# A transformer block on one core: how the MLP's normalised rows of token blocks 1 to 3 are transposed

## The chip, the cores and the metric

The kernel runs on one core of one Trainium2 chip. A core has five engines, each with an instruction queue of its own that is worked off in order: TensorE (PE in the profile; its weight loads are listed as PEld), VectorE (DVE), ScalarE (ACT), GpSimd (POOL) and SyncE (SP), which here issues nearly all DMAs. Engines wait for one another by semaphores. TensorE reads SBUF and writes PSUM; DRAM is reached by DMA only.

The metric is the device time of one execution in microseconds (us), as the median of several executions. Before the change it is 1103.45 us (three executions, 1102.35 to 1103.99).

## The reference

All tensors are float32; there are 2048 tokens of width 448.

```python
x = A_x
mod = (_silu(c) @ w_mod).reshape(c.shape[0], 6, 1, -1)
sa, ca, ga, sb, cb, gb = (mod[:, 0], mod[:, 1], mod[:, 2], mod[:, 3], mod[:, 4], mod[:, 5])
h = _layernorm(x, axis=-1) * (1 + ca) + sa
x = x + ga * _A_ref(h, A_wqkv, A_wo)          # softmax attention, 16 heads of 28
h = _layernorm(x, axis=-1) * (1 + cb) + sb
x = x + gb * _B_ref(h, B_w1, B_b1, B_w2, B_b2)
# _B_ref: y = layernorm(h); gelu(y @ w1 + b1) @ w2 + b2, with 1792 hidden units
```

The change lies in the MLP `_B_ref` at the end, between its layernorm and its first matmul. That matmul contracts over the 448 features, and TensorE contracts over partitions, so the normalised rows, which lie with one token per partition, have to be transposed to one feature per partition.

## The kernel before, in words

The kernel works in token blocks of 512 (`NB` = 4 of them, b = 0 to 3), each held as four tiles of 128 tokens, t = 0 to 3. The layernorms, projections and attention fill the first 790 us; the MLP of the four blocks follows. Each float32 operand is split into two float32r parts, a rounded `hi` and the remainder `lo`, and each product is made as three matmuls.

**The MLP loop.** The order of every engine's instructions is that in which the program is written out; there is no scheduler. The loop runs over `seq`, 56 pairs (b, i) with i = 0 to 13, one per 128 hidden units, one number n after another. A step of it emits:

- `mlp1(b, i)`: 11 matmuls of 512 columns (line 396) over the block's transposed rows `yT[b]`, in the order hi of chunks 0 to 2 twice each, lo of chunks 0 to 2, then chunk 3 twice; a GELU on ScalarE (L1394); the split into `hi` (L1397) and `lo` (L1398). The `hi` is made by ScalarE in block 0 and by VectorE in blocks 1 to 3.
- in block 0 also the rest of the attention's output projection (`tail`, with L1032) and one or two `w_prep.step()`, which load and split weight pieces (L1175 to L1209).
- one stage of the layernorm of the next block, `lnst[b + 1][0](i)`.
- `mlp2` of the step before the last (`LAG` = 2): 12 matmuls of 448 columns (L1438 to L1440) that add into four PSUM tiles. Its last step of a block, emitted at step 1 of the next block, adds the residual (L1444) into `xn` tiles and stores them (L1445).

**The layernorm of the next block** (`ln2_stages(b)`). Its `stage(i)` takes these parts at these steps: `stat(0, t)` (statistics of the block's rows) at i = t; `mid(t)` at 4 + t, which normalises into a tile of the four-buffer ring `xn` and has GpSimd multiply and add two modulation rows; `stat(1, t)` at 6 + t; `fin(t)` at 10 + t // 2, which normalises again in place (`normalise`, L217) and copies the last 64 columns a second time behind the 448 (L1129), so that the row has four full chunks of 128; `addb(t)` at 10 + t, a GpSimd addition that prepares the residual.

**The transposes** (`chunk(k)`, k = 0 to 3). At the last step of a block (i = 13, `ahead`) chunks 0 and 1 of the next block are emitted ahead of `mlp2`, chunks 2 and 3 behind it; the next instruction on TensorE is then `mlp1(b + 1, 0)`. A chunk is four TensorE transposes of 128x128 (`transposes`, L277) into a PSUM tile, a ScalarE copy that rounds to `hi` (L1155), and a VectorE subtraction that leaves `lo` (L1157, or L1159 for chunk 3, where the 64 doubled features hold `lo` in the other half of the partitions). Since TensorE's queue is in order, `mlp2` of the last two steps of block b stands behind `mlp1(b + 1, 0)` and `mlp1(b + 1, 1)`.

`slot("e1", ...)` names an SBUF buffer that holds weights of the output projection until that is done, at step 8 of block 0 at the latest.

Of the kernel before, what the change touches and what calls it, by code (L numbers as in the profile page):

```python
# [13 lines left out]
F32 = mybir.dt.float32  # L14
F32R = mybir.dt.float32r
AF = mybir.ActivationFunctionType
ALU = mybir.AluOpType
# [5 lines left out]
D = 448  # L23
# [3 lines left out]
NC = 4  # L27
# [17 lines left out]
def tile_adaln_block(ctx: ExitStack, tc: tile.TileContext, x, wqkv, wo, w1, b1, w2, b2, c, w_mod, out):  # L45
    nc = tc.nc
    pe, act, dve, pool, sp = nc.tensor, nc.scalar, nc.vector, nc.gpsimd, nc.sync
# [13 lines left out]
    def ps_tile(key, n=1):  # L61
        return ps_pools[key][1].tile([128, 512], F32, tag=key, name=nm(key), bufs=n)
# [7 lines left out]
    dr = ctx.enter_context(tc.tile_pool(name="dr", bufs=1, space=DRAM))  # L70
# [4 lines left out]
    def nm(t):  # L75
        uid[0] += 1
        return f"{t}_{uid[0]}"

    def sbt(tag, shape, dt=F32, bufs=1):
        return sb.tile(shape, dt, tag=tag, name=nm(tag), bufs=bufs)  # L80

    def slot(tag, shape, dt=F32R):
        return sb.tile(shape, dt, tag="slot_" + tag, name=nm("slot_" + tag), bufs=1)
# [24 lines left out]
    def ps_mx():  # L108
        mx_ring.append(mx_ring.pop(0))
        return ps_tile(mx_ring[-1], 1 if mx_ring[-1] == "m1" else 2)  # L110

    def ps_o():
        return ps_tile("o")
# [4 lines left out]
    def f(t):  # L118
        return t.bitcast(F32)
# [48 lines left out]
    def mod_part(k, j, n):  # L168
        if k < 3:
            return slice(0, 128), slice(j * D, (j + 1) * D)  # L170
        h, j = divmod(j, n // 2)
        return slice(64 * h, 64 * h + 64), slice(j * D, (j + 1) * D)
# [25 lines left out]
    def ln_stat(mv, t, src):  # L198
        st = sbt("st", [128, 6], bufs=2)
        dve.bn_stats(out=st, in_=src)  # L200
        dve.bn_aggr(out=mv[:, t, :], in_=st)

    def ln_rstd(mv, n):
        ve = sbt("ve", [128, 4], bufs=2)
        dve.tensor_scalar(out=ve[:, :n], in0=mv[:, :n, 1], scalar1=EPS, scalar2=None, op0=ALU.add)
        rs = sbt("rs", [128, 4], bufs=2)
        pool.tensor_tensor(out=rs[:, :n], in0=ve[:, :n], in1=neg_half[:, :n], op=ALU.pow)
        return [(mv[:, t, 0:1], rs[:, t : t + 1], rs) for t in range(n)]
# [7 lines left out]
    def normalise(dst, src, mr):  # L216
        dve.tensor_scalar(out=dst[:, :D], in0=src, scalar1=mr[0], scalar2=mr[1], op0=ALU.subtract, op1=ALU.mult)  # L217

    def xn_t():
        return sbt("xn", [128, 512], bufs=4)  # L220
# [54 lines left out]
    def transposes(p, xs, k):  # L275
        for t in range(4):
            pe.transpose(p[:, t * 128 : (t + 1) * 128], xs[t][:, k * 128 : (k + 1) * 128], ident)  # L277
# [40 lines left out]
    for k in range(NC):  # L318
        for j in range(2):
            rs_, cs = mod_part(k, j, 2)  # L320
# [94 lines left out]
    def qk_task(b, kind, g, begun=None):  # L415
        p, ts = begun or qk_terms(b, kind, g)
        if begun is None:
            mm_acc(p, ts, p1_n[3])
        emit_task(*p1_n[:3])
        if g == 0:  # L420
            tg = ("kh" if kind else "qh") + str(b)
            hi = sb.tile([128, 512], F32R, tag=tg, name=nm(tg), bufs=1)
            (kh_sb if kind else qh_sb)[(g, b)] = hi
        elif g == 1 and b < 2:

            hi = sbt("raw" if kind else "osb", [128, 512], F32R, bufs=3 if kind else 2)
            (kh_sb if kind else qh_sb)[(g, b)] = hi
        else:
            hi = sbt("hi", [128, 512], F32R, bufs=3)
        full = sbt("full", [128, 512], bufs=3)  # L430
        lo = sbt("lo", [128, 512], F32R, bufs=3)
        act.copy(full, p)

        def split():
            (act.copy if b else dve.tensor_copy)(hi, full)
            if kind == 1 and (g, b) == (0, 1):
                k_diff.append(sbt("raw", [128, 512], F32R, bufs=3))
                pool.tensor_tensor(out=k_diff[0], in0=f(hi), in1=f(kh_sb[(0, 0)]), op=ALU.subtract)
            pool.tensor_tensor(out=lo, in0=full, in1=f(hi), op=ALU.subtract)
            sl = slice(b * 512, (b + 1) * 512)  # L440
            for part, t in enumerate((hi, lo)):
                sp.dma_start(f(dscr[kind][part][g])[:, sl], f(t))

            if b < 3 or g == 0 or (kind, g) == (0, 1):
                put_spare()
            spare.append((kind, g, sl))

        return split
# [285 lines left out]


    rows = {}
    drow = dr.tile([4, D], F32, tag="drow", name="drow", bufs=1)

    mod = {}
# [65 lines left out]
    for n, i in (  # L805
# [7 lines left out]
        p, ts = firsts[n]  # L813
# [3 lines left out]
    for b in range(NB):  # L817
# [12 lines left out]
        for n, (tb, kind, g) in enumerate(tasks):  # L830
# [9 lines left out]
            k = n - (6, 4, 4, 4)[b]  # L840
# [5 lines left out]
            if kind < 2:  # L846
                fn = qk_task(tb, kind, g, firsts[n] if b == 0 and n < 3 else None)
# [12 lines left out]
            if more:  # L860
                k = n - (6, 4, 4, 4)[b]

                if b == 0 and n in (0, 1, 3, 4):
                    x = 2 * n if n < 2 else 2 * n - 2
# [237 lines left out]
    yT = {}  # L1102

    def ln2_stages(b):
        h2 = []
        ys = []

        mv = {}
        mr = {}

        def stat(which, t):
            if t == 0:
                mv[which] = sbt("mv", [128, 4, 2], bufs=2)
            ln_stat(mv[which], t, acc[b][:, t, :] if which == 0 else h2[t])
            if t == 3:
                mr[which] = ln_rstd(mv[which], 4)

        def mid(t):
            yt = xn_t()
            ys.append(yt)  # L1120
            y = yt[:, :D]
            normalise(y, acc[b][:, t, :], mr[0][t])
            pool.tensor_tensor(out=y, in0=y, in1=rows["cb"], op=ALU.mult)
            pool.tensor_tensor(out=y, in0=y, in1=rows["sb"], op=ALU.add)
            h2.append(y)

        def fin(t):
            normalise(ys[t], h2[t], mr[1][t])
            dve.tensor_copy(ys[t][:, D:512], ys[t][:, 384:D])  # L1129

        def addb(t):
            pool.tensor_tensor(out=acc[b][:, t, :], in0=acc[b][:, t, :], in1=rows["b2g"], op=ALU.add)

        plan = {}
        for t in range(4):
            plan.setdefault(t, []).append(lambda t=t: stat(0, t))
            plan.setdefault(4 + t, []).append(lambda t=t: mid(t))
            plan.setdefault(6 + t, []).append(lambda t=t: stat(1, t))
            plan.setdefault(10 + t // 2, []).append(lambda t=t: fin(t))
            plan.setdefault(10 + t, []).append(lambda t=t: addb(t))  # L1140

        def stage(i):
            for fn in plan.get(i, ()):
                fn()

        def chunk(k):
            if b not in yT:
                tiles = [
                    sb.tile([128, 512], F32R, tag=YTAGS[(7 * b + n) % len(YTAGS)], name=nm("y"), bufs=1) for n in range(7)
                ]  # L1150
                yT[b] = (lambda k: tiles[k] if k < 3 else tiles[6], lambda k: tiles[3 + k])
            p = ps_o() if b and k == 3 else ps_mx()
            transposes(p, ys, k)
            hi = yT[b][0](k)
            act.copy(hi, p)  # L1155
            if k < 3:
                dve.tensor_tensor(out=yT[b][1](k), in0=p, in1=f(hi), op=ALU.subtract)  # L1157
            else:
                dve.tensor_tensor(out=hi[64:128], in0=p[64:128], in1=f(hi)[64:128], op=ALU.subtract)  # L1159

        return stage, chunk

# [81 lines left out]
    at(28, b2_mul)  # L1244
    last0 = NKT * (NU - 1)
    lnst = [ln2_stages(b) for b in range(NB)]
    for i in range(14):
        at(last0 - 9 + i, lambda i=i: lnst[0][0](i))
# [199 lines left out]
    for n in range(len(seq) + LAG):  # L1448
        if n < len(seq):
            b, i = seq[n]  # L1450
# [54 lines left out]
```

## Time and profile before

| | |
|---|---|
| median of the runs | 1103.45 us (1102.35 to 1103.99) |
| profiled execution | 1103.82 us, span 1101.7 us, 20731 instructions |
| PE busy | 1094.3 us (99% of the span) |
| DVE busy | 798.9 us (73%) |
| ACT busy | 697.3 us (63%) |
| POOL busy | 196.8 us (18%) |
| DMA | 82.67 MB, mean 75 GB/s |
| first matmul of the MLP (L396 on a `y` tile) | starts 792.1 us into the span |

Times in all views are microseconds from the start of the span of one profiled execution. In a row of the timeline the columns are the start, the length, the engine, the line of the kernel, the operation, the tiles as out<-in, the shape, the count, and in brackets how long the engine stood idle before and what ended that. Matmul lengths overlap: the pace of TensorE is read from the distance between starts. In a row of grouped instructions the number behind the bar is the group's busy time and the mean length of one in ns, then the idle time before it. A row of the windows gives, for a stretch, its length and the busy time of each engine, then the granted TensorE clock, the busy share of the 16 DMA engines and the GB/s that they moved. `SPq` is a DMA being issued by SyncE; the row's length is the issue, not the transfer.

### The profile page before, as it was taken

To read this page: it belongs to the slowest core of one execution; us is meant where nothing else is said; L and a number is where in the kernel's file an instruction comes from. 1 tells how busy PE (TensorE), PEld (TensorE's weight loads), DVE (VectorE), ACT (ScalarE), POOL (GpSimd) and SP (SyncE) were. 2 spreads that over 40 slices of the span, in tenths; PEclk is the share of its full clock that TensorE was granted. 3 is DMA by queue.
4 is the path that set the end of the run, shared out by engine and by line. 5 is a ranking of instruction groups with operands and counts; after the bars stand their busy time and mean duration, and the time that the engine had idled before them with its cause. 6 is when DMAs were issued, how large, how long until landed. Compare 5 with 4: busy or idle time off the path is not lost.

```text
span 1101.7 us, 20731 instructions
## 1 busy us (share of the span) xinstructions
PE 1094.3 (99%) x8303; PEld 665.3 (60%) x8303; DVE 798.9 (73%) x1382; ACT 697.3 (63%) x883; POOL 196.8 (18%) x201
## 2 busy tenths in 40 slices
PE   9999999999999999999999999999999999999998
PEld 6756675444444444444444444554488888888887
DVE  6968788999999989988888888574655644444322
ACT  4655667888888888888888888678933411211210
POOL 1543332210000000000000000116123214023000
PEclk9999999999999999999999999999999999999999
DMA  9553354221222201231211313111451000000000
GB/s 311 199 191 106 99 183 138 60 64 33 75 76 61 76 28 40 69 102 47 69 48 38 98 42 99 57 31 59 146 144 50 27 34 1 15 20 1 34 1 34
DMA packets 51094, 82.67 MB, mean 75 GB/s; under 512 B 13327, under 2 KB 19878, under 8 KB 50986
## 3 DMA queue, kind: packets, MB, share of 16 engines
q1 hardware_dynamic: 50514, 80.61, 23.9%
q8 instruction: 65, 1.06, 0.4%
q10 hardware_dynamic: 148, 0.46, 0.1%
q0 software_dynamic: 336, 0.28, 0.1%
q14 instruction: 31, 0.25, 0.1%
HBM read 56.25 MB, written 26.75 MB: 75 GB/s over the span
## 4 chain that ended last, share of the span: by engine, by line
PE 97%; DVE 1%; ACT 0%; DMA 0%; issue 0%; ACTq 0%; DVEq 0%
PE s L1348 23%; PE o L1303 23%; PE m L396 17%; PE pa L396 9%; PE m L476 8%; PE s L1439 3%; PE s L1440 3%; PE s L1438 3%; PE s L476 2%; PE t L1439 1%; PE t L1440 1%; PE t L1438 1%; PE o L277 1%; DVE mxp L481 0%; PE ma L476 0%; PE m L277 0%
## 5 line engine op out<-in xcount | busy, mean ns | idle before, releaser
L481 DVE TENSOR_REDUCE mxp<-m 128x1 f32<-128x512 f32 x555 | 359.9, 686 | 64.7 <-PE m L476 46.9
L1348 PE MATMUL s<-slot_b,slot_a 28*128 28x512 f32 (+1 forms) x3072 | 356.7, 423 | 0.0
L1348 PEld LDWEIGHTS s<-slot_b,slot_a 28*128 28x128 f32 (+1 forms) x3072 | 211.2, 183 | 175.8 <-ACT slot_c L1361 96.4
L476 PE MATMUL m<-kh,qh 28*128 28x512 f32 x607 | 227.0, 468 | 0.4 <-DVE mxp L481 0.3
L1361 ACT ACTIVATE slot_c<-s 128x1024 f32<-128x1024 f32 x170 | 174.8, 1028 | 51.5 <-PE s L1348 50.8
L1303 PE MATMUL o<-slot_c,v 128*32 128x512 f32 x680 | 178.9, 605 | 0.0
L1394 ACT ACTIVATE full<-m,b_col 128x512 f32<-128x512 f32 x56 | 38.6, 689 | 205.3 <-PE m L396 188.5
L686 DVE TENSOR_REDUCE mxp<-s 128x2 f32<-128x1024 f32 x107 | 131.2, 1226 | 5.0
L1303 PE MATMUL o<-slot_c1h,v 128*32 128x512 f32 x512 | 134.7, 605 | 0.0
L1303 PE MATMUL o<-slot_c0h,v 128*32 128x512 f32 x508 | 133.6, 605 | 0.0
L1361 ACT ACTIVATE slot_c1h<-s 128x1024 f32<-128x1024 f32 x128 | 130.7, 1021 | 0.0
L1361 ACT ACTIVATE slot_c0h<-s 128x1024 f32<-128x1024 f32 x127 | 130.5, 1027 | 0.0
L1397 DVE CAST hi<-full 128x512 fp32r<-128x512 f32 x42 | 18.6, 443 | 121.1 <-ACT full L1394 121.1
L1361 ACT ACTIVATE slot_d<-s 128x1024 f32<-128x1024 f32 x86 | 88.4, 1028 | 25.2 <-PE s L1348 24.9
L476 PEld LDWEIGHTS m<-kh,qh 28*128 28x128 f32 x607 | 90.8, 182 | 15.2 <-DVE mxp L481 13.3
L1303 PE MATMUL o<-slot_d,v 128*32 128x512 f32 x344 | 90.5, 605 | 0.4 <-ACT osb L1267 0.4
L1061 POOL TENSOR_TENSOR osb<-osb,osb 128x512 f32<-128x512 f32 x16 | 20.6, 1284 | 363.5 <-DMA osb<-drec 247.1
L1398 DVE TENSOR_TENSOR lo<-full,hi 128x512 fp32r<-128x512 f32 x56 | 43.0, 768 | 26.6 <-ACT hi L1397 22.6
L396 PE MATMUL m<-y,slot_a 128*128 128x512 f32 x160 | 60.7, 395 | 0.0
L481 DVE TENSOR_REDUCE mxp<-ma 128x1 f32<-128x512 f32 x61 | 39.5, 682 | 13.2 <-PE m L476 8.0
L1303 PEld LDWEIGHTS o<-slot_c,v 128*32 128x32 f32 x680 | 24.5, 108 | 39.0 <-issue 36.4
L650 DVE CUSTOM_DVE_ANT_0 slot_d0i<-m,slot_d0i 128x512 f32<-128x512 f32 x54 | 37.3, 691 | 14.3 <-PE m L476 11.6
(351 smaller groups left out, 1835.7 us busy)
## 6 DMA issues: line engine op xcount, KB each, us to landing
slot_b<-d SPq DMA_DIRECT2D x32, 256.0 KB
slot_a<-d SPq DMA_DIRECT2D x32, 256.0 KB
d<-lo SPq DMA_DIRECT2D x28, 256.0 KB
d<-hi SPq DMA_DIRECT2D x16, 256.0 KB
osb<-drec SPq DMA_DIRECT2D x15, 256.0 KB
out_dram<-xn SPq DMA_DIRECT2D x16, 224.0 KB
raw<-in_B_w_dram SPq DMA_DIRECT2D x14, 224.0 KB
qh<-d SPq DMA_DIRECT2D x12, 256.0 KB
```

The costliest lines, as they stand in the source:

```text
L396: pe.matmul(p, a, b, start=(i == 0), stop=(i == len(terms) - 1))
L476: pe.matmul(m, qh_sb[(g, qt)][js, i * 128 : (i + 1) * 128], k[js, :], start=True, stop=True)
L481: dve.tensor_reduce(out=mxp[(g, qt)][:, i, j, cch : cch + 1], in_=m, op=ALU.max, axis=AX.X)
L686: dve.tensor_reduce(out=mxp[(g, qt)][:, i, j : j + 2, cch], in_=t, op=ALU.max, axis=AX.X)
L1303: pe.matmul(o[32 * j : 32 * j + 32, :], v_sb[kt // 4][:, kt % 4, 4 * g + j, :], p[j // 2][:, j % 2, :], start=(kt == 0), stop=(kt == NKT - 1),
L1348: pe.matmul(s2[:, jj, :], ks[rows_, kp, kc], qs[rows_, qp, :], start=(term == 0), stop=(term == 2))
L1361: act.activation(pt[hf], s2, AF.Exp, scale=SCALE)
L1394: act.activation(gf, p, AF.Gelu_apprx_tanh, bias=b1_col[:, i : i + 1])
L1398: dve.tensor_tensor(out=glo, in0=gf, in1=f(ghi), op=ALU.subtract)
L1438: pe.matmul(pp, ghi[:, ts], w_hi, start=(m == 0), stop=False)
L1439: pe.matmul(pp, ghi[:, ts], w_lo, start=False, stop=False)
L1440: pe.matmul(pp, glo[:, ts], w_hi, start=False, stop=(m == NFT - 1))
```

## The change

For blocks 1 to 3 TensorE no longer transposes. VectorE turns each normalised tile in 32x32 blocks (`turn(t)`: one instruction per tile, 128x448, into the buffer `e1`). Four DMAs (`send`), one for each group of 32 partitions, write the result to a DRAM tensor `y_dr` of 448 x 512, in runs of 128 floats. Five DMAs (`fetch`) read it back with one feature per partition into four `xn` tiles: one each for chunks 0 to 2, two for chunk 3, whose 64 rows are read twice. The fetches can start when all four sends have landed. `chunk(k)` then takes its rows from that tile instead of PSUM; the tokens come back in another order, and the access patterns of the ScalarE copy and the VectorE subtraction put them right in runs of 32. The copy of 64 columns in `fin` is left to block 0 alone.

The steps: for block 1 all parts of the layernorm stay where they were, `turn` is at steps 11 and 12 of block 0, `send` at 12, `fetch` at 13, the chunks at 13 as before. For blocks 2 and 3 the two statistics, `mid` and `fin` move ahead, two tiles per step (`stat(0)` at 0 and 1, `mid` at 2 and 3, `stat(1)` at 4 and 5, `fin` at 6 and 7), `turn` is at 7 and 8, `send` at 8, `fetch` at 9, the chunks still at 13. Block 0 is transposed as before.

```diff
     rows = {}
+    y_dr = dr.tile([D, 512], F32, tag="y_dr", name="y_dr", bufs=1)
...
+        turned = []
+
         def fin(t):
             normalise(ys[t], h2[t], mr[1][t])
-            dve.tensor_copy(ys[t][:, D:512], ys[t][:, 384:D])
+            if not b:
+                dve.tensor_copy(ys[t][:, D:512], ys[t][:, 384:D])
+
+        def turn(t):
+            if t == 0:
+                turned.append(slot("e1", [128, 14, 4, 32], F32))
+            dve.transpose(turned[0][:, :, t, :], ys[t][:, :D].rearrange("p (c j) -> p c j", j=32))
+
+        def send():
+            for r in range(4):
+                sp.dma_start(
+                    y_dr.rearrange("(c i) (r n) -> r i c n", i=32, r=4)[r],
+                    turned[0][32 * r : 32 * r + 32].rearrange("i c t j -> i c (t j)"),
+                )
+
+        def fetch():
+            for k in range(NC):
+                turned.append(xn_t())
+                for h in range(1 if k < 3 else 2):
+                    rs_ = slice(0, 128) if k < 3 else slice(64 * h, 64 * h + 64)
+                    sp.dma_start(turned[-1][rs_], y_dr[128 * k : min(128 * k + 128, D), :])
...
         for t in range(4):
-            plan.setdefault(t, []).append(lambda t=t: stat(0, t))
-            plan.setdefault(4 + t, []).append(lambda t=t: mid(t))
-            plan.setdefault(6 + t, []).append(lambda t=t: stat(1, t))
-            plan.setdefault(10 + t // 2, []).append(lambda t=t: fin(t))
-            plan.setdefault(10 + t, []).append(lambda t=t: addb(t))
+            at_stage = (t, 4 + t, 6 + t, 10 + t // 2, 10 + t) if b < 2 else (t // 2, 2 + t // 2, 4 + t // 2, 6 + t // 2, 10 + t)
+            for i, fn in zip(at_stage, (lambda t=t: stat(0, t), lambda t=t: mid(t), lambda t=t: stat(1, t), lambda t=t: fin(t), lambda t=t: addb(t))):
+                plan.setdefault(i, []).append(fn)
+            if b:
+                plan.setdefault((11 if b < 2 else 7) + t // 2, []).append(lambda t=t: turn(t))
+        if b:
+            plan.setdefault(12 if b < 2 else 8, []).append(send)
+            plan.setdefault(13 if b < 2 else 9, []).append(fetch)
...
-            p = ps_o() if b and k == 3 else ps_mx()
-            transposes(p, ys, k)
             hi = yT[b][0](k)
+            lo = yT[b][1](k) if k < 3 else hi
+            rs_ = slice(0 if k < 3 else 64, 128)
+            if b:
+                p = turned[1 + k].rearrange("p (r t j) -> p r t j", r=4, t=4)
+                hi, lo = (x.rearrange("p (t r j) -> p r t j", r=4, t=4) for x in (hi, lo))
+            else:
+                p = ps_mx()
+                transposes(p, ys, k)
             act.copy(hi, p)
-            if k < 3:
-                dve.tensor_tensor(out=yT[b][1](k), in0=p, in1=f(hi), op=ALU.subtract)
-            else:
-                dve.tensor_tensor(out=hi[64:128], in0=p[64:128], in1=f(hi)[64:128], op=ALU.subtract)
+            dve.tensor_tensor(out=lo[rs_], in0=p[rs_], in1=f(hi)[rs_], op=ALU.subtract)
```

## The prediction

> **What bounds the kernel now.** I read the page first, busy shares and then the chain that ended last.
>
> ```profile
> span 1101.7 us, 20731 instructions
> PE 1094.3 (99%) x8303; PEld 665.3 (60%) x8303; DVE 798.9 (73%) x1382; ACT 697.3 (63%) x883; POOL 196.8 (18%) x201
> ...
> PE 97%; DVE 1%; ACT 0%; DMA 0%; issue 0%; ACTq 0%; DVEq 0%
> ```
>
> TensorE is busy for 99% of the span and carries 97% of the chain. So an instruction taken off TensorE is worth its place in TensorE's stream, and any wait of TensorE is lost in full: its queue is in order and has no spare time to give back. The other engines' work counts only if it is late for TensorE. The place to look at is therefore the boundary between two blocks, in the timeline. Block 0 to block 1:
>
> ```profile
> 874.27 1.03 PE L277 MATMUL m<-ident,xn 128*128 128x128 f32 x8
> ...
> 875.06 0.45 PE L1438 MATMUL s<-slot_d0i,hi 128*128 128x448 f32 x1
> ...
> 875.36 0.36 PE L1439 MATMUL s<-slot_b1h,hi 128*128 128x448 f32 x1
> ...
> 875.56 0.36 PE L1440 MATMUL s<-slot_d0i,lo 128*128 128x448 f32 x1
> ...
> 877.59 0.60 PE L277 MATMUL m<-ident,xn 128*128 128x128 f32 x4
> ...
> 878.99 0.50 PE L396 MATMUL m<-y,slot_b 128*128 128x512 f32 x1 [0.36 <-DVE y L1157]
> ...
> 879.33 0.40 PE L396 MATMUL m<-y,slot_a 128*128 128x512 f32 x1
> ...
> 879.56 0.40 PE L396 MATMUL m<-y,slot_b 128*128 128x512 f32 x1
> ```
>
> The pace is 0.20 us for a 448-column matmul (875.36 to 875.56) and 0.23 us for one of 512 (879.33 to 879.56). The 12 matmuls of `mlp2` alone would take 12 x 0.203 = 2.43 us. The first eight transposes begin at 874.27; the second matmul behind them starts at 875.36 where 874.27 + 0.20 would do: 0.89 us. From 877.59, where the next eight begin, to 879.33, less one pace, is 1.51 us, of which 0.36 us is a wait for VectorE. Together 2.40 us. The next two boundaries:
>
> ```profile
> 946.73 1.03 PE L277 MATMUL m<-ident,xn 128*128 128x128 f32 x8
> 946.98 0.69 ACT L1394 ACTIVATE full<-m,b_col 128x512 f32<-128x512 f32 x1 [4.32 <-PE m L396]
> ...
> 948.24 0.69 DVE L1398 TENSOR_TENSOR lo<-full,hi 128x512 fp32r<-128x512 f32 x1
> ...
> 951.16 0.40 PE L396 MATMUL m<-y,slot_a 128*128 128x512 f32 x1
> ```
>
> ```profile
> 1018.57 1.03 PE L277 MATMUL m<-ident,xn 128*128 128x128 f32 x8
> ...
> 1023.00 0.40 PE L396 MATMUL m<-y,slot_a 128*128 128x512 f32 x1
> ```
>
> Both take 4.43 us from the first transpose to the second matmul of `mlp1`; less 2.43 and 0.23 that is 1.77 us each. All 48 transposes hold TensorE for 2.40 + 1.77 + 1.77 = 5.9 us. That is all the change can gain.
>
> **Blocks 2 and 3.** Turn, send and fetch are issued at steps 7 to 9, the chunks at 13; a step is 23 matmuls, 11 x 0.234 + 2.43 = 5.0 us, so some 20 us lie between fetch and use, and the DMAs cost nothing. If that cover were gone the price would be that of block 1 below. SP has no loads left there, so its nine DMAs per block have the queue to themselves; the stores of the block before are issued at step 1. GpSimd, in whose queue `mid`'s additions now come two steps sooner, holds nothing else there until `addb`. `mid` at step 2 takes `xn` tiles whose stores began one step earlier; VectorE may wait there a microsecond, behind it stand `hi` and `lo` of the next step, which TensorE needs two steps later: hidden. The 1.77 us go. A little comes back: ScalarE's four copies start behind the GELU (946.98 + 0.69), VectorE's four subtractions behind L1398 (948.24), at about 0.6 us apart the last ends near 951.4; TensorE, 1.77 us earlier, starts `mlp1` at 946.73 + 2.43 = 949.16 and wants it nine matmuls on, at 951.27. I charge 0.25 us (0 to 0.8). Gain 1.5 us each, 3.0 in all (2.0 to 3.5).
>
> **Block 1: when the turned rows are ready to leave.** Here `turn` is at steps 11 and 12, `send` at 12, `fetch` at 13, and the chunks are wanted at the end of step 13. VectorE's own rows:
>
> ```profile
> 868.45 0.51 DVE L217 TENSOR_SCALAR xn<-xn,mv,rs 128x448 f32<-128x448 f32 x1
> ...
> 872.70 0.63 DVE L1209 TENSOR_TENSOR slot_e<-full,slot_e 128x448 fp32r<-128x448 f32 x1 [0.63 <-ACT slot_e L1208]
> 875.85 0.69 DVE L1398 TENSOR_TENSOR lo<-full,hi 128x512 fp32r<-128x512 f32 x1 [2.52 <-ACT hi L1397]
> ```
>
> ```profile
> L525 DVE STREAM_TRANSPOSE full<-m x16: 200/202/211, 161.4 to 745.8; 128x32 f32<-128x32 f32 x16
> ```
>
> A turn of 32 columns takes 0.20 us, nearly all of it the start; for 448 columns L217, the same shape from SBUF to SBUF, takes 0.51: I take 0.6 us (0.5 to 1.1, twice that). Turns 0 and 1 fit behind L217. Turns 2 and 3 stand behind the weight split L1209, which ends at 873.33: done at about 874.45 (874.3 to 875.5). They end ahead of 875.85 and delay nothing on VectorE; the four dropped 64-column copies of a block are off the path too.
>
> **Block 1: the way through DRAM.** The last output stores move the same 896 KB and are the nearest row for the sends:
>
> ```profile
> 1096.79 0.33 SPq L1445 DMA_DIRECT2D out_dram<-xn  x1
> ...
> 1097.50:1098.00 0.50, 0.34 (x2) 0.00 (x0) 0.50 (x2) 0.00 (x0) 0.00 (x0) 1.00 0.74 269
> ...
> 1100.00:1100.50 0.50, 0.00 (x0) 0.00 (x0) 0.00 (x0) 0.00 (x0) 0.00 (x0) 1.00 0.19 65
> ...
> L1501 SPq DRAIN x3: 7/7/7, 1100.9 to 1101.2; - x3
> ```
>
> Issue at 1096.79, data from about 1097.6 to 1100.1, SP free of the wait at 1100.9: 0.8 + 2.5 + 0.8 = 4.1 us. But those are runs of 1792 bytes from 128 partitions; a send takes runs of 512 bytes from 32. The nearest row for few partitions is the staging of the attention output, eight DMAs of 56 KB from 28 partitions each:
>
> ```profile
> 359.87 1.61 SPq L1082 DMA_DIRECT2D o<-hi  x4
> 361.58 1.64 SPq L1082 DMA_DIRECT2D o<-lo  x4
> ...
> 361.30:361.80 0.50, 0.50 (x8) 0.00 (x0) 0.41 (x2) 0.50 (x1) 0.00 (x0) 1.00 0.53 131
> ```
>
> 131 GB/s with the DMA engines 53% busy, paced by its issue. At 131 GB/s the sends' data take 7.0 us, at 131 / 0.53 = 247 GB/s 3.7 us, at the stores' rate 2.5. I take 4.2, near the middle row plus half a microsecond for the shorter runs. [...]
>
> ```profile
> SPq L1056 <- DMA drec<-den: 27.0, 15, 3.1
> ...
> 787.18 1.82 SPq L1175 DMA_DIRECT2D raw<-in_B_w_dram  x1
> ...
> 791.47 0.43 DVE L1187 CAST slot_v<-raw 128x512 fp32r<-128x512 f32 x1 [2.16 <-DMA raw<-in_B_w_dram]
> ```
>
> An 8 KB write to DRAM makes SP wait 27.0 / 15 = 1.8 us behind its issue, so I take 1.1 us from the last byte to the landing (0.8 to 1.8). The sends have landed 0.05 + 0.8 + 4.2 + 1.1 = 6.15 us after 874.45, at 880.6; their four issues, about 0.5 us each, lie inside. A fetch of 256 KB is bounded above by the weight load, 791.47 - 787.18 = 4.3 us, of which 1.82 is its issue, and below by 0.8 + 0.7 + 0.5 = 2.0; I take 2.3, 0.8 to the first byte, 0.7 of data, 0.8 to land: 882.95. ScalarE's copy of chunk 0 and the semaphores are 0.65: TensorE can start `mlp1(1, 0)` at 883.6 (881.3 to 886.7). It is free at 874.27 + 2.43 = 876.70. It idles for about 6.9 us (4.6 to 10). Everything behind on its queue, `mlp2` of block 0's last two steps included, waits with it; the chunk copies also block ScalarE and VectorE, but what stands behind them there needs the same matmuls. Against 879.10, when `mlp1(1, 0)` starts now, it is 4.5 us later.
>
> The four chunks then come 0.7 us apart, the last in two halves; with a copy and a subtraction behind it (0.6 + 0.7) chunk 3 is ready about 3.1 us after chunk 0, where the tenth matmul wants it after 9 x 0.234 = 2.1: 1.0 us more (0.5 to 1.5). Block 1 so far: +5.5 us.
>
> **The clock after the idle time.** TensorE's longest waits are these, and the first is the start of the kernel, so what follows a long idle time is not shown; but TensorE is slow when it begins:
>
> ```profile
> PE pa L311 <- POOL cst L127: 1.4, 1, 1.4
> PE o L1303 <- ACT osb L1267: 0.4, 1, 0.4
> ...
> L321 PE MATMUL pa<-slot_c,slot_d x4: 954/955/956, 8.1 to 8.9; 128*32 128x448 f32 x4
> ...
> L321 PE MATMUL pa<-slot_c,slot_d x4: 539/540/540, 10.9 to 11.2; 128*32 128x448 f32 x4
> ```
>
> The same form takes 0.955 us at 8.1 us and 0.54 us at 10.9, with a recorded clock of 1.00 in both: a slow stretch of some 8 us from the first matmul at 1.4 us, at about half pace. If the idle time brings it back, the loss is between 0 and half of 8 us, less the 1.0 us of chunk waits that slow matmuls hide: 0 to 3. I take 1.5, since the work here is denser than at the start. [...]
>
> **The sum.** Block 1: +4.5 + 1.0 + 1.5 = +7.0; blocks 2 and 3: -3.0; net +4.0 us. The profiled execution's own time is 1103.82, its span 1101.7, 2.1 us around it; the median is 1103.45, 0.4 us below it. On the median: 1107.4 us, 0.36% more. About 0.2% (2.2 us) is what a measurement of this kernel can tell from no change.
>
> **Rivals.**
>
> - The round trip is short: turns done at 874.3, sends at the stores' 4.1 us, fetch 2.0, chunk waits 0.5, clock unaffected. `mlp1` starts at 881.3, 2.2 us later than now, plus 0.5, less 3.5 in blocks 2 and 3: -0.8 us, 1102.7, not slower. For it speaks the stores' row; against it the o<-hi row and the mean of 1.8 us for a small write. It decides where the way from turn to `mlp1` stays under about 7.5 us.
> - The idle time leaves the clock alone: +5.5 - 3.0 = +2.5 us, 1105.9. For it: a recorded clock of 1.00 everywhere; against it the two L321 rows.
> - The sends run at the o<-hi pace of 131 GB/s, or the turns cost double: 2.8 us or 1.0 us more and the clock stays slow for longer, net about +7 to +8, 1111. Against it: that row is held back by issue.
> - The change doesn't do its work sooner in blocks 2 and 3, because a wait I have taken as hidden is not (the `xn` ring, GpSimd slowing VectorE): their 3.0 us shrink towards 0, net +6 to +7. Against it: two steps, 10 us, of slack.
>
> **How the numbers follow.** Forecast 0.50, short round trip 0.17, warm clock 0.18, slow sends or turns 0.10, blocks 2 and 3 without gain 0.05. Faster needs less than 1101.2, below the short trip's -0.8 by another 1.4 us: 0.07, all from that case's spread. Within 0.2%: the other 0.10 of that case, a third of the warm clock (0.06), a little of the forecast (0.05): 0.21. Slower: 0.72. The range from 1102.8 to 1111.0 runs from the short trip to the slow sends; the forecast's own is 1105 to 1110.
>
> **What would show it.** Right: no L277 behind block 0; TensorE idle some 7 us once, before `mlp1(1, 0)`, ended by ScalarE's copy and behind it by a DMA; no idle time over 0.8 us at the other two boundaries; matmuls after the idle time at about twice the pace for some microseconds. Wrong: an idle time under 4 us (the trip), matmuls at 0.23 us straight after it (the clock), idle time inside blocks 1 to 3 (the ring), a turn over 1.1 us.

## The result and the profile after

The changed kernel takes 1108.24 us (median of five, 1107.58 to 1108.38) against 1103.45 before: 1.0044 times as long, 95% interval 1.0029 to 1.0058. The profiled execution has a span of 1105.9 us against 1101.7, 4.2 us more. The page of the changed kernel, busy shares and the chain that ended last:

```profile
span 1105.9 us, 20699 instructions
PE 1091.5 (99%) x8255; PEld 661.1 (60%) x8255; DVE 807.0 (73%) x1382; ACT 697.7 (63%) x883; POOL 198.7 (18%) x201
...
PE 96%; DVE 2%; DMA 1%; ACT 1%; issue 0%; SPq 0%; ACTq 0%; DVEq 0%
```

TensorE is busy for 2.8 us less and the span is longer, so it must wait somewhere. Its list of waits names the place, and there is only one that is new:

```profile
PE m L396 <- ACT y L1187: 7.4, 1, 7.4
```

L1187 is the chunk's copy to `hi`. The timeline around it, first TensorE at the boundary from block 0 to block 1 (L1467 to L1469 are `mlp2`), then the other engines (L1138 is `turn`, L1142 `send`, L1152 `fetch`; the buffer `e1` is listed as `slot_e`):

```profile
874.20 0.37 PE L1467 MATMUL s<-slot_d0i,hi 128*128 128x448 f32 x1
...
876.44 0.37 PE L1469 MATMUL s<-slot_d0i,lo 128*128 128x448 f32 x1
884.20 0.79 PE L396 MATMUL m<-y,slot_b 128*128 128x512 f32 x1 [7.39 <-ACT y L1187]
...
886.11 0.63 PE L396 MATMUL m<-y,slot_b 128*128 128x512 f32 x1
886.53 0.63 PE L396 MATMUL m<-y,slot_a 128*128 128x512 f32 x1
...
888.11 0.40 PE L396 MATMUL m<-y,slot_a 128*128 128x512 f32 x1
888.34 0.39 PE L396 MATMUL m<-y,slot_b 128*128 128x512 f32 x1
888.57 0.37 PE L1467 MATMUL s<-slot_e,hi 128*128 128x448 f32 x1
```

```profile
872.63 0.62 DVE L1238 TENSOR_TENSOR slot_e<-full,slot_e 128x448 fp32r<-128x448 f32 x1 [0.63 <-ACT slot_e L1237]
873.17 1.16 DVE L1138 STREAM_TRANSPOSE slot_e<-xn 128x448 f32<-128x448 f32 x2
874.36 3.03 SPq L1142 DMA_DIRECT2D y_dr<-slot_e  x4
...
880.52 2.43 SPq L1152 DMA_DIRECT2D xn<-y_dr  x5
883.53 0.62 ACT L1187 CAST y<-xn 128x512 fp32r<-128x512 f32 x1 [5.93 <-DMA xn<-y_dr]
```

The last turns end behind the weight split at 874.3. The four sends are issued from 874.36, and SP can issue the first fetch at 880.52, when all have landed. The first chunk is there at 883.5. TensorE, which has had nothing to start since 876.64 and whose last matmul ended at 876.81, starts at 884.20. Then its matmuls come 0.42 us apart (886.11 to 886.53) in place of 0.23, until about 888. The windows show why; the last three columns are the granted clock, the DMA engines' share and GB/s:

```profile
875.50:876.00 0.50, 0.50 (x4) 0.47 (x3) 0.23 (x1) 0.24 (x1) 0.00 (x0) 1.00 0.97 177
...
878.00:878.50 0.50, 0.00 (x0) 0.00 (x0) 0.25 (x1) 0.00 (x0) 0.00 (x0) 1.00 1.07 279
...
880.70:881.20 0.50, 0.00 (x0) 0.00 (x0) 0.00 (x0) 0.00 (x0) 0.00 (x0) 0.91 0.00 0
881.20:884.20 3.00, 0.00 (x1) 0.00 (x1) 0.02 (x1) 0.62 (x1) 0.00 (x0) 0.50 0.87 297
...
887.50:888.00 0.50, 0.50 (x3) 0.40 (x2) 0.00 (x0) 0.00 (x0) 0.00 (x0) 0.57 0.00 0
```

A mean of 0.91 over 0.5 us puts the halving of the clock at 881.1, 4.3 us after TensorE's last matmul ended; it is back at 887.9, 3.7 us after TensorE resumed. The slow stretch is 6.8 us long, and 3.1 of them lay in the idle time. The next boundary, block 1 to 2, goes through without a wait until the last chunk:

```profile
953.76 0.37 PE L1467 MATMUL s<-slot_d0i,hi 128*128 128x448 f32 x1
...
956.21 0.39 PE L396 MATMUL m<-y,slot_b 128*128 128x512 f32 x1
...
958.54 0.50 PE L396 MATMUL m<-y,slot_a 128*128 128x512 f32 x1
958.88 0.40 PE L396 MATMUL m<-y,slot_b 128*128 128x512 f32 x1
959.11 0.37 PE L1467 MATMUL s<-slot_e,hi 128*128 128x448 f32 x1
```

The account closes. The rows of the kernel before that end the same stretches:

```profile
881.64 0.37 PE L1438 MATMUL s<-slot_e,hi 128*128 128x448 f32 x1
```

```profile
953.48 0.37 PE L1438 MATMUL s<-slot_e,hi 128*128 128x448 f32 x1
```

From the first instruction behind the last `mlp1` of a block to the first `mlp2` matmul behind `mlp1(b + 1, 0)`, the boundary to block 1 took 7.37 us before (874.27 to 881.64) and takes 14.37 now: +7.00. The boundaries to blocks 2 and 3 took 6.75 (946.73 to 953.48 for the first) and take 5.35 (953.76 to 959.11): -1.40 each. 7.00 - 2.80 = 4.2 us, the difference of the spans.

### The profile page after: what moved, and what is told of

The parts are those of the page before. It is cut to its first block, busy times and chain, and to the rows that moved or that the text cites. A ratio compares the mean times of both kernels' runs of the same rounds, so it can differ in the third digit from the quotient of the medians.

```text
span 1105.9 us, 20699 instructions
## 1 busy us (share of the span) xinstructions
PE 1091.5 (99%) x8255; PEld 661.1 (60%) x8255; DVE 807.0 (73%) x1382; ACT 697.7 (63%) x883; POOL 198.7 (18%) x201
## 4 chain that ended last, share of the span: by engine, by line
PE 96%; DVE 2%; DMA 1%; ACT 1%; issue 0%; SPq 0%; ACTq 0%; DVEq 0%
PE s L1377 23%; PE o L1332 23%; PE m L396 16%; PE pa L396 9%; PE m L476 8%; PE s L1468 3%; PE s L1467 3%; PE s L1469 3%; PE s L476 2%; PE t L1468 1%; PE t L1469 1%; PE t L1467 1%; PE o L277 1%; DVE mxp L481 0%; PE ma L476 0%
## 5 line engine op out<-in xcount | busy, mean ns | idle before, releaser
L1427 DVE TENSOR_TENSOR lo<-full,hi 128x512 fp32r<-128x512 f32 x56 | 46.1, 823 | 25.8 <-ACT hi L1426 21.6
L396 PE MATMUL m<-y,slot_a 128*128 128x512 f32 x160 | 61.6, 401 | 0.2
L476 PE MATMUL s<-kh,qh 28*128 28x512 f32 x214 | 48.1, 444 | 0.0
```

The costliest lines, as they stand in the source:

```text
L396: pe.matmul(p, a, b, start=(i == 0), stop=(i == len(terms) - 1))
L476: pe.matmul(m, qh_sb[(g, qt)][js, i * 128 : (i + 1) * 128], k[js, :], start=True, stop=True)
L1427: dve.tensor_tensor(out=glo, in0=gf, in1=f(ghi), op=ALU.subtract)
```

## The experiments

Each kernel was compared with the kernel before on the same chip. Since the MLP starts 791.0 to 792.6 us into the span of the profiled executions, the table also gives the MLP's own length in the profiled execution, from the first to the last matmul of `mlp1`. In kernels to which two lines were added further up, L396 and L1187 have become L398 and L1189.

| kernel | median us | before, us | ratio (95%) | MLP, us |
|---|---|---|---|---|
| before | 1103.45 | | | 298.1 |
| changed | 1108.24 | 1103.45 | 1.0044 (1.0029 to 1.0058) | 302.3 |
| blocks 2 and 3 only | 1100.56 | 1103.01 | 0.9976 (0.9967 to 0.9985) | 295.8 |
| block 1 only | 1110.17 | 1103.01 | 1.0063 (1.0051 to 1.0076) | 305.2 |
| busy while waiting | 1107.24 | 1103.01 | 1.0034 (1.0021 to 1.0046) | 301.7 |
| wait filled | 1103.69 | 1103.01 | 1.0003 (0.9994 to 1.0011) | 297.5 |
| block 1 sooner | 1100.43 | 1103.02 | 0.9975 (0.9966 to 0.9984) | 295.2 |
| sooner norms only | 1103.94 | 1103.02 | 1.0009 (1.0000 to 1.0018) | 298.2 |
| all late | 1125.47 | 1103.02 | 1.0194 (1.0179 to 1.0210) | 320.5 |
| two queues, far groups (one execution) | 1106.67 | 1103.02 | | 301.0 |
| two queues, near groups (one execution) | 1108.89 | 1103.04 | | 304.1 |
| block 1 sooner, chunks first | 1097.84 | 1103.04 | 0.9955 (0.9941 to 0.9968) | 292.6 |

**The two halves of the change.** `VIA_DRAM` and `EARLY` are the blocks that are turned through DRAM and whose norms are sooner.

```diff
+VIA_DRAM = (2, 3)      # second kernel: (1,)
+EARLY = (2, 3)         # second kernel: ()
...
-            if b:
+            if b in VIA_DRAM:
                 p = turned[1 + k].rearrange("p (r t j) -> p r t j", r=4, t=4)
```

> Block 1 goes back to TensorE's transposes at its old steps; blocks 2 and 3 stay with the turn through DRAM and the sooner norms. Theory (the loss is all block 1's round trip, the gain all the transposes of blocks 2 and 3): TensorE's stream gains 1.77 - 0.33 = 1.44 us at each of two boundaries, -2.9 us against before, about 1100.6; no idle time of TensorE over 0.5 us in the MLP. Rival (the sooner norms or the DMA traffic of blocks 2 and 3 cost time inside the blocks, and block 1 is blamed for it): -1 us or no gain at all, 1102.5 to 1103.5.

> Only block 1 goes through DRAM, with its turn at steps 11 and 12; blocks 2 and 3 keep TensorE's transposes and the old steps. Theory: the idle time of 7.4 us and the slow first matmuls stay as they are in the changed kernel, +7.0 us against before, about 1110.4. Rival (parts of the loss lie elsewhere): +5 us or less. The sum of this and the run with blocks 2 and 3 alone should give the change's +4.2 to +4.8 us; if not, the two parts act on one another.

With blocks 2 and 3 alone the kernel is 2.5 us faster than before, with block 1 alone 7.2 us slower; together 4.7, the change's 4.8. In the trace of the first no wait is left at the boundaries but the old one of TensorE's transposes in block 1; that of the second has the same long wait as the changed kernel:

```profile
PE m L398 <- DVE y L1190: 0.4, 1, 0.4
```

```profile
PE m L398 <- ACT y L1189: 7.6, 2, 7.4
```

At the boundaries themselves the first kernel has -1.40 twice and the second +7.35 once. So the loss is block 1's and the gain is that of the other two, and no effect of the one on the other is seen.

**The sooner norms by themselves.**

```diff
+VIA_DRAM = ()
+EARLY = (2, 3)
```

> The kernel before with nothing but the sooner statistics, mid and fin in blocks 2 and 3; all blocks transposed by TensorE. Theory: no effect on TensorE's stream, 1103.2, within 0.1% of before. Rival (moving them helps or harms by itself, through the xn ring or GpSimd slowing VectorE): more than 1 us either way.

The MLP takes 298.2 us, before 298.1. The medians differ by 0.9 us with an interval that begins at no change; the profiled MLP shows no place for it, so whether there is an effect of that size stays open. All three boundaries take what they took before. So no gain of the sooner norms by themselves is seen; they make room for the trip.

**All three blocks late.**

```diff
+VIA_DRAM = (1, 2, 3)
+EARLY = ()
```

> The changed kernel with the norms of blocks 2 and 3 at the old steps, so that all three blocks turn at steps 11 and 12, send at 12 and fetch at 13. Theory (what decides is the time between send and use): each of blocks 2 and 3 gets an idle time like block 1's, somewhat shorter since no weight split stands ahead of its last turns (about 1.0 to 1.5 us), so 5 to 6 us lost per block instead of 1.44 gained: 13 to 15 us more than the changed kernel, 1121 to 1123. Rival (block 1 alone is slow, because of weight loads or the projection in block 0): about 1108 to 1112.

```profile
PE m L398 <- ACT y L1189: 19.0, 5, 7.1
```

All three boundaries now have the wait: 7.1 us to block 1, 5.4 and 5.7 to blocks 2 and 3. That block 1 alone is slow is thereby excluded; it is the time between send and use. The time is 2.5 us above the expected range. The windows show the half clock behind the first wait from 880.27 to 890.5:

```profile
880.00:880.50 0.50, 0.00 (x0) 0.00 (x0) 0.00 (x0) 0.00 (x0) 0.00 (x0) 0.77 0.00 0
...
890.50:891.00 0.50, 0.50 (x4) 0.46 (x3) 0.50 (x1) 0.00 (x0) 0.00 (x0) 0.99 0.00 0
```

TensorE, which resumed at 883.21, was slow for 7.3 us there, and for 6.2 and 5.5 us behind the other two waits, where the changed kernel had 3.7. That accounts for the excess in part; it was not taken apart further.

**Idle time and clock taken apart.** TensorE is kept busy while it waits:

```diff
             mlp2(*seq[n - LAG])
+        if ahead and b == 0:
+            keep = ps_mx()
+            for j in range(30):
+                pe.matmul(keep, w1t[0][0](0)[:, :128], w1t[0][0](1)[:, :512], start=(j == 0), stop=(j == 29))
```

> The changed kernel with thirty further matmuls of 512 columns behind the last mlp2 that TensorE can still do before mlp1 of block 1 (30 x 0.234 = 7.0 us), whose result nothing reads: TensorE stays busy while it waits for the rows. Theory (the idle time slows the clock, and slow matmuls hide that chunks 2 and 3 come late): granted clock 1.00 throughout, mlp1 of block 1 at a pace of 0.23 us but with waits of about 1.0 us for the last chunk; it ends near 3.6 us after its start in place of 4.4, so -0.8 us against the changed kernel, about 1107.4. Rival A (the chunks are there in time): the whole 1.8 us come back, 1106.4. Rival B (the first matmuls are slow for another reason than the idle time, for instance the new tiles): the pace stays at 0.43 us, no change in time.

```profile
875.99 7.00 PE L1497 MATMUL m<-slot_b 128*128 128x512 f32 x30
883.28 0.50 PE L396 MATMUL m<-y,slot_b 128*128 128x512 f32 x1 [0.29 <-ACT y L1187]
883.62 0.40 PE L396 MATMUL m<-y,slot_a 128*128 128x512 f32 x1
...
885.13 0.50 PE L396 MATMUL m<-y,slot_b 128*128 128x512 f32 x1 [0.27 <-ACT y L1187]
...
886.71 0.50 PE L396 MATMUL m<-y,slot_a 128*128 128x512 f32 x1 [0.16 <-DVE y L1188]
887.05 0.39 PE L396 MATMUL m<-y,slot_b 128*128 128x512 f32 x1
887.28 0.37 PE L1467 MATMUL s<-slot_e,hi 128*128 128x448 f32 x1
```

```profile
882.00:884.00 2.00, 1.71 (x7) 0.78 (x5) 0.69 (x1) 1.17 (x2) 0.00 (x0) 1.00 0.96 344
```

The clock stays at 1.00 there and pairs of matmuls run 0.23 us apart, so the slow pace does come from the idle time, not from new tiles. But `mlp1` still takes 4.00 us (883.28 to 887.28) against 4.37 at half clock and 2.57 with all its data there: TensorE now waits for chunks 1, 2 and 3 one after another. So the two rivals fall: the chunks were not there in time, and the pace was not slow for another reason. By these two executions the clock's own share of the 1.8 us is about 0.4, and the other 1.4 are chunks that come late, which slow matmuls hide. In this execution the last copy came some 0.3 us later behind the first than in the changed kernel, so the changed kernel's own last subtraction gives a second figure:

```profile
885.07 2.19 DVE L1188 TENSOR_TENSOR y<-xn,y 128x512 fp32r<-128x512 f32 x3 [0.20 <-ACT y L1187]
```

It ends at 887.26. Here the last two matmuls of `mlp1` end their stretch 0.62 us behind that subtraction (886.66 to 887.28); by that estimate an `mlp1` at the full clock would be done at 887.88 in the changed kernel, where it was done at 888.57: 0.7 us for the clock. So the clock's share is 0.4 to 0.7 us. The MLP is 0.6 us shorter than the changed kernel's, and so is the median beside its own kernel before, a little less than the 0.8 expected.

**The wait filled with work that stands behind it.**

```diff
+        if ahead and b == 0:
+            for k in range(2, NC):
+                lnst[b + 1][1](k)
+            for m in range(NFT - 1 - LAG, NFT):
+                mlp2(0, m)
+            continue
-        if n >= LAG:
+        if n >= LAG and n - LAG not in (NFT - 2, NFT - 1):
             mlp2(*seq[n - LAG])
```

> The changed kernel with mlp2 of block 0's last two steps put ahead of mlp1 of block 1, so that 24 matmuls (4.9 us) of the work that stands behind the wait run during it. Theory: the idle time falls from 7.4 to about 2.5 us, too short for the clock to fall (it fell 4.5 us after TensorE stopped), and mlp1 loses about 1.0 us to the late chunks: 4.9 + 0.8 = 5.7 us less than the changed kernel, about 1102.5, near before. Rival (the clock falls after shorter idle times too, or the block's end is late elsewhere, with its output adds now waiting for the chunks on VectorE): -4 us or less, 1104 and above.

```profile
882.84 0.56 PE L396 MATMUL m<-y,slot_b 128*128 128x512 f32 x1 [2.65 <-ACT y L1187]
883.19 0.63 PE L396 MATMUL m<-y,slot_a 128*128 128x512 f32 x1
883.62 0.63 PE L396 MATMUL m<-y,slot_b 128*128 128x512 f32 x1
```

```profile
882.00:883.00 1.00, 0.16 (x1) 0.16 (x2) 0.18 (x1) 0.83 (x2) 0.00 (x0) 1.00 0.90 301
883.00:885.00 2.00, 1.85 (x5) 0.83 (x6) 1.31 (x3) 1.05 (x3) 0.00 (x0) 0.54 0.30 95
...
886.50:887.00 0.50, 0.50 (x3) 0.41 (x3) 0.50 (x2) 0.00 (x0) 0.00 (x0) 0.94 0.00 0
```

The idle time fell to 2.65 us as expected, and the MLP by 4.8 us. But the clock halved all the same, near 883.15, after TensorE had resumed at 882.84, and stayed so for 3.4 us, half as long as in the changed kernel; the expectation that 2.65 us are too short was wrong, and the rival was right in this. The profiled execution, 1102.00, is also 1.7 us faster than the median: by the medians, each beside its own kernel before, the gain over the changed kernel is 4.1 us where 5.7 were expected. Of the 11 executions, ten have a mean clock of 0.997 or 0.998; the one with 1.000 is the fastest, 1101.68. The four with 0.998, as the profiled one has, average 1102.9 us, the six with 0.997, as the profiled changed kernel has with its 6.8 us, 1104.2. That a longer slow stretch costs the difference is likely, but only one of them was traced.

**Block 1 early enough.**

```diff
+VIA_DRAM = (1, 2, 3)
+EARLY = (1, 2, 3)
...
+            if b in VIA_DRAM:
+                plan.setdefault((8 if b < 2 else 7) + t // 2, []).append(lambda t=t: turn(t))
...
+            plan.setdefault(9 if b < 2 else 8, []).append(send)
+            plan.setdefault(10 if b < 2 else 9, []).append(fetch)
```

> The changed kernel with block 1's norms two tiles per step as in blocks 2 and 3 and its turn at steps 8 and 9, send at 9, fetch at 10 (the buffer is free of weights from step 8 on). Theory (only the lateness of block 1's send costs): some 15 us lie between fetch and use, the idle time goes, and block 1 gains about 2.1 us (its old 2.40 less about 0.3): 2.1 + 2.9 = 5.0 us less than before, about 1098.5. Rival (VectorE and GpSimd are too full in block 0, where weights are split and the projection is added, so that hi and lo of the hidden rows come late for TensorE): idle times of TensorE inside block 0, 1100 to 1104.

```profile
876.81 0.56 ACT L1239 CAST slot_e<-full 128x448 fp32r<-128x448 f32 x1 [1.29 <-DVE full L1237]
877.28 2.18 ACT L1189 CAST y<-xn 128x512 fp32r<-128x512 f32 x4
...
877.95 0.51 PE L398 MATMUL m<-y,slot_b 128*128 128x512 f32 x1 [1.36 <-ACT y L1189]
```

The long wait is gone, but 1.4 us are left at the boundary, which takes 7.21 us (873.98 to 881.19) where it took 7.37 before: block 1 gains 0.16 us there where about 2.1 were expected. The MLP is 0.6 us shorter than with blocks 2 and 3 alone, but the medians, 1100.43 and 1100.56, show no gain that could be told from noise. No data are late: ScalarE's four copies stand behind the weight split's cast (L1239), which itself waited for VectorE. Nothing waited inside block 0, so the rival's reason does not hold either.

**The chunks first.** This kernel also emits the four chunks right behind the GELU of the block's last step, in place of the end of that step:

```diff
+        if i == NFT - 1 and b + 1 < NB:
+            for k in range(NC):
+                lnst[b + 1][1](k)
         (dve.tensor_copy if b else act.copy)(ghi, gf)
```

> The run with block 1 sooner, with one thing more: at a block's last step the four chunk copies and subtractions are emitted right behind the GELU, ahead of that step's hi and lo, of the weight split and of mlp2. Theory (what was left at the boundaries, 1.4 + 0.2 us at block 1 and 0.33 at blocks 2 and 3, is ScalarE's and VectorE's order of work, not data that are late): no idle time of TensorE over 0.15 us behind the start of the MLP, 2.2 us less than that run, about 1098.3. Rival (hi and lo of the last hidden rows, now behind the chunks, become late for mlp2): idle time ahead of mlp2 instead, no gain.

```profile
876.26 0.37 PE L1474 MATMUL s<-slot_d0i,lo 128*128 128x448 f32 x1
876.47 0.39 PE L398 MATMUL m<-y,slot_b 128*128 128x512 f32 x1
```

`mlp2` and `mlp1` of block 1 now stand 0.21 us apart, and TensorE waits nowhere in the MLP. Each of the three boundaries takes 5.00 us, which is what its matmuls need. The MLP takes 292.6 us, 5.5 less than before, of the 5.9 that the transposes held; the kernel takes 1097.84 us, 0.9955 of before, and is faster than both the kernel before and the changed one.

**What holds the sends.** In the changed kernel the first two sends moved 173 to 177 GB/s with the DMA engines 97 to 99% busy, later ones up to 279. Two kernels issue block 1's sends from two queues and differ in which groups of 32 partitions run together:

```diff
-            for r in range(4):
-                sp.dma_start(
+            for r in (0, 2, 1, 3):        # second kernel: (0, 1, 2, 3)
+                (act if b == 1 and r in (2, 3) else sp).dma_start(   # second kernel: (1, 3)
```

> The changed kernel with block 1's sends issued from two queues, groups 0 and 1 of 32 partitions from SyncE and groups 2 and 3 from ScalarE, so that partitions below and above 64 are read at the same time. Theory (a send from partitions of one half is held at about 177 GB/s, as the first two sends were, and the halves add up): the data take about 3.3 us in place of 4.7, the idle time shrinks by 1 to 1.5 us to about 6. Rival (512-byte runs hold each DMA engine, whatever the partitions): no difference to the next run, 4 to 4.7 us of data.

> The same two queues as in the run with two far groups, but groups 0 and 2 from SyncE and 1 and 3 from ScalarE, so that the two DMAs that run together read partitions of the same half, first below 64, then above. In the far run the data took about 3.5 us at 257 to 330 GB/s. Theory (the half of the partitions holds the rate): the data take about 5 us, 917504 bytes at 177 GB/s, and the idle time is that of the changed kernel, 7 to 7.6 us, in spite of the faster issue. Rival (the second queue alone made the far run faster): as fast as the far run, idle about 5.9 us.

Windows of the first, with groups on both sides of partition 64 together:

```profile
875.50:876.00 0.50, 0.50 (x4) 0.47 (x3) 0.00 (x0) 0.47 (x2) 0.00 (x0) 1.00 1.12 272
...
876.50:877.00 0.50, 0.00 (x0) 0.00 (x0) 0.50 (x2) 0.00 (x0) 0.00 (x0) 1.00 1.14 330
```

and of the second, with both groups on the same side:

```profile
875.00:875.50 0.50, 0.50 (x4) 0.33 (x2) 0.00 (x0) 0.50 (x1) 0.00 (x0) 1.00 0.98 177
...
876.00:876.50 0.50, 0.00 (x0) 0.00 (x0) 0.50 (x2) 0.00 (x0) 0.00 (x0) 1.00 0.97 169
```

The data take about 3.5 us (874.9 to 878.4) in the first and 4.7 (874.15 to 878.85) in the second, which is the single queue's time. So by one execution of each the second queue alone did not shorten the data, and groups from both sides of partition 64 together did, as the theory expected. Whether the side they are read from is the reason is left open, since the pairs also differ in where they write: the near ones fill neighbouring 512-byte runs of `y_dr`, the far ones do not, and that was not tried apart, nor what runs of 512 bytes cost by themselves. The idle time falls from 7.4 to 5.9 us; in the second it is 7.0. The second kernel's MLP is still 1.8 us longer than the changed kernel's: its third chunk came late (TensorE waited 0.7 us more inside `mlp1`) and its clock halved at 879.7, with a mean of 0.995 over the run, where the changed kernel has 0.997.

## Why the prediction was right

The forecast of 1107.4 us was 0.8 below the measured time, and its account held: what was gained, what was waited for, and that the clock fell. That block 1's +7.0 us came out to the digit is luck, since two terms were wrong against one another: `mlp1` started 5.17 us later than before where 4.5 were charged, and 1.83 us were lost behind that where 2.5 were charged.

- **What the transposes held.** 1.77 us at each of blocks 2 and 3; gone in full, with 0.33 us come back at the last chunk where 0.25 was charged. The net 1.40 us per block (1.5 forecast) comes out again at both boundaries of the kernel with blocks 2 and 3 alone, whose median gains 2.5 us.
- **The way to TensorE.** The sends left at 874.36 (874.45 forecast) and had landed 6.16 us later (6.15). Within that, two terms were off against one another, which is luck too: 4.7 us of data from 875.2 to 879.9 against 4.2, and 0.6 behind the last byte against 1.1. The half microsecond for the shorter runs in the 4.2 was the author's estimate; no run shows it by itself. The fetch to ScalarE's start took 3.0 us (880.52 to 883.53) against 2.3: the term of the sum that was too small. TensorE idled for 7.4 us (6.9) and started at 884.20 (883.6).
- **Chunks and clock.** 1.0 + 1.5 us were charged, 1.80 measured (4.37 for an `mlp1` that needs 2.57). The clock did fall, but the two terms were mis-sized: the late chunks by themselves cost 1.1 to 1.4 us, and the clock's own share is 0.4 to 0.7, not 1.5. The forecast took 0 to 3 us, less 1.0 us of chunk waits already, for the fall; 3.1 of the 6.8 us at half clock lay in the idle time and cost nothing, and slow matmuls hid more waiting than the 1.0. The slow start of the kernel, on which the term rested, was a likeness only: its rows have a recorded clock of 1.00, these 0.50.
- **The rivals.** The short trip (it decides under 7.5 us from turn to `mlp1`) did not occur: 874.3 to 884.2 is 9.9. The warm clock is refuted by the windows, which show 0.50. Slow sends and slow turns did not occur either: the sends moved 197 GB/s from 875.5 to 879.5, not 131, and two turns took 1.16 us, not 2.2. That blocks 2 and 3 would not gain, or that the ring or GpSimd would make TensorE wait inside them, is refuted by the two halves. VectorE's L217 and L1427 did take up to 1.5 us each there while GpSimd was busy, as single ones did before (1.34 and 1.45), unseen by TensorE.

## What to carry to other kernels

Work taken off the bounding engine is worth its place there only if what replaces it is ready in time: the trip through DRAM gained 1.4 us per block in blocks 2 and 3 when it was sent five steps ahead of its use, and lost 7 us per block when it was sent one step ahead (22.4 us for all three). So place the producer by its whole latency, here 10 us from the last turn to the first matmul, and then look at the order of the queues that hand the data over, which was worth another 2.6 us. Where a wait of the bounding engine cannot be avoided, move independent work in front of the waiting instruction, and do not count the clock's fall twice with the lateness of the data behind it. In the kernel with the wait filled that order was worth 4.1 us.

## What the runs showed of the hardware that was not expected

A TensorE that stopped for 2.65 us, in the kernel with the wait filled, had its clock halved, 3.0 us after its last matmul ended and 0.3 us after it had resumed. A stop of 1.4 us, in the kernel with block 1 sooner, left the run's mean clock at 1.000 and the matmuls behind it 0.23 us apart where their data were there (878.81 to 879.04). In the other kernels whose windows cover the fall it came 3.1 us (two far groups, at 879.53) to 4.3 us (the changed kernel, at 881.1) after the last matmul's end.

The half clock lasted 3.4 us in the kernel with the wait filled, 6.8 in the changed kernel and 10.2 at the first wait with all blocks late (880.27 to 890.5), after stops of 2.65, 7.4 and 7.1 us. So two stops of nearly the same length had slow matmuls of different duration behind them: 3.7 us in the changed kernel and 7.3 at the first wait with all blocks late. What sets the moment of the fall and the length of the half clock was not shown.

Two DMAs from groups of 32 partitions on the side below partition 64 shared 169 to 186 GB/s (near groups, 874.5 to 876.5), and two above it 191 to 220; one from each side reached 257 to 330 (far groups, 875.5 to 878.0). A half microsecond at 267 in the kernel with near groups lies where one pair gave way to the other, and the changed kernel's single queue rose from 157 to 279 and 236 at the same point, when the first half of the data had left. These are one execution of each kernel, and what makes the rates differ was not shown.
